# A state-space layer and two MLPs in one kernel: some decay matrices by ScalarE's exponential, the opening units reordered, the whole order planned anew

## The chip, the cores and the metric

One core of a Trainium2 chip runs the kernel. Its engines are TensorE (PE, matmul; PEld is its weight load), VectorE (DVE), ScalarE (ACT) and GpSimd (POOL); SyncE (SP) issues nearly all DMA transfers. The metric is device time in microseconds (us) of one execution, smaller is better.

## What is computed

```python
# 4 batches x 8 heads x 768 steps, head_dim 32, state 16, chunks of 32
L = np.exp(cum[:, :, :, None] - cum[:, :, None, :]) * causal   # cum: running sum of log a
y_intra = einsum('bhij,bhjd->bhid', (C @ B.T) * L, x)
y_inter = einsum('bhin,bhnd->bhid', C, state) * np.exp(cum)[..., None]
state = decay_full * state + sum(B x decay_from_j)
...
xn = x / sqrt(mean(x * x) + 1e-6) * rms_g              # 3072 tokens x 256
x = (silu(xn @ w_gate) * (xn @ w_val)) @ w_out         # d_ff 1536
out = softplus(x @ w_in) @ w_out2                      # d_ff 2048
```

All of it is in float32. Each product of the two MLPs is made from three matmuls on split operands: high part times high part, low times high, high times low.

## The kernel before

The state-space layer is cut into 24 *units* of 128 steps of one batch (8 heads each), four units to a *block* of 512 tokens; units 0 to 3 are block 0. A unit needs a decay matrix for each of its 8 heads (two tiles of 128 x 512, index `s`), which `unit` makes with a `tensor_tensor_scan` on DVE (L566: running products of `a`, restarted by a row of the identity). PE makes the unit's C·B scores into two PSUM banks of the tag `a` (`scores`), DVE multiplies them into the decays (`decay`, L615), PE makes the unit's output and new state (`products`), ACT squares it and scales it by the RMS gain, and `norm` makes 1/rms: a mean by PE (`msum`), a power by POOL, a broadcast by PE (`rspread`), a product on DVE (L783), then the split into high part (ACT, L358) and low part (DVE or POOL, L365). There are only two `a` banks, so the scores of the next unit wait for both decays of this one. For units 0 to 3 the values of `a` are spread over partitions by PE (`spread`, tiles `p<-st,small`) into a `p` bank; there are four of those, one of them held by the filler matmuls until the MLP begins.

Then comes SwiGLU on block 0 (f runs over 12 slices of 128 columns: `wg`, `wv` by `three_pass`, then `wo` in `back`), on block 1, the second MLP (`wi`, `wp`) on both, and so on over six blocks. One front of SwiGLU for one f is 12 matmuls of 512 columns. A weight chunk holds two values of f. It comes by DMA (`wr`) and is unpacked by ACT (`zz`, L447), DVE (L450), ACT (high part, L454) and DVE (low part, L456). Units 4 to 23 run between the matmuls of the MLPs.

Every operation is first recorded with a cost per engine (`Plan.op`). `Plan.emit` then runs a list scheduler twice. The first run is over the opening operations that carry a time by hand (table `LEAD`, `FIRST`); it yields times that they hold later. The second is over everything, by fixed ranks, and its order is the program's order on each engine. Idle time on PE before the MLP is filled with *filler* matmuls (`p<-mean`), which keep PE's clock up; their number and places are part of the fixed program order.

Of the kernel before, what the change touches and what calls it, by code (L numbers as in the profile page):

```python
# [26 lines left out]
NATIVE, SPREAD = 8, 4  # L27
NORMS = {0: [1, 1, 1, 1]}
# [11 lines left out]
FIRST = [(12.05, 14.4, 15.0, 17.3), (12.1, 15.2, 16.2, 20.4)]  # L40

LEAD = dict(
    spread0=(-0.6, 0.0, 2.6, 6.1), spread1=(-0.4, 1.5, 3.7, 9.6), scores=(-0.2, 4.9, 8.4, 12.1), products=(6.0, 9.5, 13.5, 15.3),
    msum=(7.9, 11.1, 15.2, 16.9), rspread=(9.55, 13.2, 17.3, 18.9),
    scan0=(0.0, 2.28, 5.75, 9.3), scan1=(1.14, 4.6, 8.1, 11.95), decay0=(3.4, 6.9, 10.4, 13.3), decay1=(4.0, 7.5, 11.0, 13.9),
    scale=(2.6, 6.0, 9.6, 13.1), norm=(11.6, 14.5, 18.3, 19.4),
    square=(7.3, 10.8, 14.5, 16.3), gains=(7.6, 11.1, 14.9, 16.6), mean=(8.7, 11.9, 16.15, 17.65), state=(8.8, 12.0, 17.7, 19.0),
    power=(8.9, 12.2, 17.3, 18.3), high=(12.2, 15.1, 18.9, 19.9), low=(12.9, 15.6, 18.8, 20.0))

W_LEAD, T0, U_LEAD, U_GAP, U_GAP0, U1, U1_GAP, B_LEAD, EPI = 50, 50, 115, 8, 4, 10, 14, 50, 40  # L50

SLIP = 100
# [25 lines left out]
class Plan:  # L78
# [3 lines left out]
    def __init__(self, latency):  # L82
        self.ops, self.bufs, self.latency = [], [], latency
        self.last_w, self.readers, self.seq = {}, {}, {}
        self.now = None
# [44 lines left out]
    def emit(self):  # L130
        lead = [i for i, o in enumerate(self.ops) if i in self.seq]
        due = {}
        self.run(lead, {}, due, True)
        for fn in self.run(range(len(self.ops)), due, {}):
            fn()

    def run(self, which, due, times, warm=False):
# [64 lines left out]
        while todo:  # L202
# [10 lines left out]
            for e in engines:  # L213
                able = []
                turn = lane[e][at[e]] if at[e] < len(lane[e]) else None
                for i in cand[e]:
                    if i in seq and i != turn:
                        continue
# [3 lines left out]
                    if i not in seq and turn is not None:  # L222
                        until = due[turn] + SLIP
                        if i in spare:
# [3 lines left out]
                    able.append((t, i not in seq, ops[i][1], i))  # L228
                while able:
# [3 lines left out]
                    end = t + ops[i][0][e][0]  # L233

                    later = False
                    for e2, way in ops[i][0].items():
                        if e2 != e:
                            ns, t2 = way[0], start(i, e2)
                            t2 += sum(ops[j][0][e2][0] for j in cand[e2]
                                      if len(ops[j][0]) == 1 and ops[j][1] < rank and ready[j] <= t2)  # L240
# [9 lines left out]
            times[i] = t  # L250
            for e2 in ops[i][0]:
                cand[e2].discard(i)
            if i in seq:
                at[e] += 1
            end = t + ns
# [34 lines left out]
def tile_ssd_then_swiglu_then_softplus_mlp(  # L290
# [84 lines left out]
    cst_sb = const.tile([P, -(-(sbuf_at // 4 + P + 1 + KD) // 64) * 64 - sbuf_at // 4], F32, name="cst_sb")  # L375
    ident4 = const.tile([P, 4 * P], F32, name="ident4")
    ident = ident4[:, 0:P]
    mask = cst_sb[:, 0:P]
    zeros = cst_sb[:, P:P + 1].to_broadcast([P, P])
    small = const.tile([P, 64], F32, name="small")  # L380
    g_sb, mhalf = cst_sb[:, P + 1:P + 1 + KD], small[:, 0:1]
    mean = const.tile([P, 64], F32, name="mean")[:, 0:1]
    sel = small[:, 4 * SPREAD:8 * SPREAD].bitcast(F32R)
# [693 lines left out]
```

## Time and profile before

| | us |
|---|---|
| runs of the kernel: median of three | 603.28 (601.46 to 604.17) |
| the profiled execution, its own time | 604.33 |
| its span, first to last instruction | 601.3 |
| PE busy in the span | 595.0 |
| DVE, ACT busy | 351.2, 309.5 |
| first MLP matmul starts at | 30.03 |

PE's instructions follow each other nearly without a gap, so "busy" does not say how much of it is useful: fillers count as busy, and so does a matmul at half clock. In the rows, a matmul of 512 columns is shown as 0.38 us long, but the next starts after about 0.215.

### The profile page before, as it was taken

The numbers are of one execution on the slowest core, as the hardware profiler recorded it, in microseconds if no ns is written. First come the engines' busy times: TensorE is split into PE (matmuls) and PEld (weight loads), VectorE is DVE, ScalarE is ACT, GpSimd is POOL, SyncE is SP. The second block draws the span as 40 slices with busy tenths as digits, with TensorE's granted clock in tenths as the row PEclk, the third lists the DMA queues.
The fourth block names the chain that finished last, engine by engine and source line by source line (L and its number), as shares of the span: only waits on it lengthen the run. The fifth ranks groups of instructions, "written<-read, shape, count | busy, mean of one in ns | idle before, by whom it ended". The sixth has DMA issues, their size and how long they took to land.

```text
span 601.3 us, 8773 instructions
## 1 busy us (share of the span) xinstructions
PE 595.0 (99%) x3377; PEld 513.7 (85%) x3377; DVE 351.2 (58%) x561; ACT 309.5 (51%) x547; POOL 20.0 (3%) x41
## 2 busy tenths in 40 slices
PE   9999999999999999999999999999999999999997
PEld 7888888888888888888888888888888888888885
DVE  6899997888683246695433779755333433322222
ACT  2666665768565445354555344665433333644543
POOL 3300000000000000000000000000000000000000
PEclk9899999999999999999999999999999999999999
DMA  6567768476710015111346533300100000000000
GB/s 210 187 206 246 248 240 245 159 241 214 232 48 36 1 43 178 42 57 35 132 173 207 163 109 88 120 1 0 37 0 1 0 2 1 0 1 0 36 1 35
DMA packets 33433, 59.74 MB, mean 99 GB/s; under 512 B 3120, under 2 KB 14960, under 8 KB 33392
## 3 DMA queue, kind: packets, MB, share of 16 engines
q1 hardware_dynamic: 33248, 58.93, 30.1%
q8 instruction: 26, 0.43, 0.3%
q10 hardware_dynamic: 144, 0.26, 0.1%
q14 instruction: 15, 0.12, 0.1%
HBM read 47.45 MB, written 11.73 MB: 98 GB/s over the span
## 4 chain that ended last, share of the span: by engine, by line
PE 94%; DVE 3%; DMA 1%; issue 0%; ACT 0%; POOL 0%; DVEq 0%; ACTq 0%
PE p L322 53%; PE t L322 35%; PE a L322 6%; DMA wr<-in_w 1%; DVE hw L365 1%; DVE wr L450 0%; DVE s L834 0%; DVE ab L566 0%; DVE xxl L783 0%; POOL xxl L365 0%; DVE xc L730 0%; DVE xxl L615 0%; DVE wol L456 0%; DVE s L359 0%; DVE wvl L456 0%
## 5 line engine op out<-in xcount | busy, mean ns | idle before, releaser
L365 DVE TENSOR_TENSOR hw<-s,hw 128x512 fp32r<-128x512 f32 x164 | 112.8, 690 | 144.0 <-ACT hw L358 83.3
L358 ACT ACTIVATE hw<-s 128x512 fp32r<-128x512 f32 x164 | 103.0, 631 | 98.9 <-DVE s L834 73.5
L322 PE MATMUL t<-hw,wph 128*128 128x512 f32 x384 | 114.7, 380 | 0.1
L846 ACT ACTIVATE s<-p 128x512 f32<-128x512 f32 x96 | 56.8, 598 | 78.7 <-PE p L322 77.6
L834 DVE TENSOR_TENSOR s<-s,p 128x512 f32<-128x512 f32 x72 | 49.2, 684 | 60.9 <-PE p L322 54.7
L322 PE MATMUL t<-hw,woh 128*128 128x512 f32 x272 | 82.3, 383 | 1.0 <-DVE hw L365 0.9
L322 PEld LDWEIGHTS t<-hw,wph 128*128 128x128 f32 x384 | 72.3, 189 | 11.0 <-ACT hw L358 0.5
L322 PE MATMUL p<-xxh,wih 128*128 128x512 f32 x192 | 72.8, 379 | 0.0
L322 PE MATMUL p<-xxl,wih 128*128 128x512 f32 x192 | 72.8, 379 | 0.0
L322 PE MATMUL p<-xxh,wil 128*128 128x512 f32 x192 | 72.8, 379 | 0.0
L322 PE MATMUL t<-hw,wpl 128*128 128x512 f32 x192 | 72.8, 379 | 0.0
L830 ACT ACTIVATE s<-p 128x512 f32<-128x512 f32 x72 | 42.8, 594 | 49.3 <-PE p L322 43.6
L322 PEld LDWEIGHTS t<-hw,woh 128*128 128x128 f32 x272 | 50.6, 189 | 9.8 <-DVE hw L365 1.8
L322 PE MATMUL p<-xxh,wgh 128*128 128x512 f32 x144 | 55.0, 382 | 0.0
L322 PE MATMUL p<-xxh,wvh 128*128 128x512 f32 x144 | 54.9, 381 | 0.0
L322 PE MATMUL p<-xxh,wvl 128*128 128x512 f32 x144 | 54.6, 379 | 0.0
L322 PE MATMUL p<-xxl,wvh 128*128 128x512 f32 x144 | 54.6, 379 | 0.0
L322 PE MATMUL p<-xxh,wgl 128*128 128x512 f32 x144 | 54.6, 379 | 0.0
L322 PE MATMUL p<-xxl,wgh 128*128 128x512 f32 x144 | 54.6, 379 | 0.0
L322 PE MATMUL t<-hw,wol 128*128 128x512 f32 x136 | 51.5, 379 | 0.0
L566 DVE TENSOR_TENSOR_SCAN ab<-ab,ident 128x512 f32<-128x512 f32 x40 | 48.7, 1219 | 2.0 <-DMA ab<-a_clip 2.0
L322 PEld LDWEIGHTS p<-xxh,wil 128*128 128x128 f32 x192 | 36.3, 189 | 5.1
(131 smaller groups left out, 753.3 us busy)
## 6 DMA issues: line engine op xcount, KB each, us to landing
wr<-in_w SPq DMA_DIRECT2D x34, 512.0 KB, 4.6
ab<-a_clip SPq DMA_DIRECT2D x20, 512.0 KB, 4.5
parts<-wr SPq DMA_DIRECT2D x16, 512.0 KB, 3.3
xc<-in_xc SPq DMA_DIRECT2D x20, 256.0 KB
st<-parts SPq DMA_DIRECT2D x16, 256.0 KB, 4.8
cz<-parts SPq DMA_DIRECT2D x32, 128.0 KB, 3.7
out_y<-s SPq DMA_DIRECT2D x11, 256.0 KB, 2.1
wr<-in_bc SPq DMA_DIRECT2D x8, 256.0 KB, 3.4
```

The costliest lines, as they stand in the source:

```text
L322: pe.matmul(out=o, lhsT=l, rhs=r, start=start, stop=stop, skip_group_check=True)
L358: ways = {"act": (act_ns(n), lambda: act.activation(out=out(), in_=in_(), func=ACTF.Copy)), "dve": (dve_ns(n, sbuf), lambda: dve.tensor_co ...
L365: return lambda: eng.tensor_tensor(out=out(), in0=in_(), in1=f32(hi()), op=ALU.subtract)
L566: DVE(512, rank[0], lambda t=t, d=d: dve.tensor_tensor_scan(out=t(), data0=d(), data1=ident4, initial=0.0, op0=ALU.mult, op1=ALU.add), dk ...
L830: ACT(n, rank - EPI, lambda: act.activation(out=s()[:, 0:n], in_=ps[0]()[:, 0:n], func=ACTF.Silu), [ps[0]], [s, "table"] if new_table else ...
L834: DVE(n, rank - EPI, lambda: dve.tensor_tensor(out=s()[:, 0:n], in0=s()[:, 0:n], in1=ps[1]()[:, 0:n], op=ALU.mult), [s, ps[1]], [s], port= ...
L846: ACT(n, rank - EPI, lambda: act.activation(out=s()[:, 0:n], in_=hp()[:, 0:n], func=ACTF.Softplus), [hp], [s, "table"] if new_table and f ...
```

## The change

- **Exponentials.** For five of the eight decay tiles of units 0 to 3 (`EXPS`: the second tile of units 0, 1 and 2, both of unit 3) the scan on DVE and the spread on PE go. In their place the logarithms of `a` are taken once (ACT, Ln), summed along the steps by one short scan (DVE), split into high and low parts, and PE makes for each tile all differences of sums in one `p` bank (`differences`: one matmul of 512 columns, four of 128, one of 512 with bf16 operands that puts -4096 where the matrix has to be zero). ACT takes Exp of it, 128 x 512.
- **Loads and tables.** Two small loads of `a` and the load of the constants are issued from ACT's queue, no longer SP's. The table loaded first holds Ln and Exp; the one with Silu is loaded at the end of the lead (one load more in all).
- **First units.** In the first run of the scheduler the times by hand no longer fix the order: of two operations that compete for an engine the one goes first whose order gives the shorter longest way to the end (`first`, `way`).
- **Whole order.** The second run is made eight times; after each, `refine` sets ranks anew from the due times of the MLP's matmuls, and the order with the earliest last matmul is kept.
- **Three passes.** `three_pass` now does high x high and high x low for both k first, low x high last. The number of MLP matmuls, 2448, stays.

```diff
+EXPS, NEVER = {(0, 1), (1, 1), (2, 1), (3, 0), (3, 1)}, -4096.0
...
+SILU = 15.0
+PASSES, MARGIN, MLP, DMA_WAIT = 8, 1.0, 768, 3000
...
+            for (_, old, n), (_, new, _) in zip(row, row[row[0][2]:]):
+                for i in old:
+                    after[i].add(new[0])
...
+        for _ in range(40):
+            for i in reversed(lead):
+                self.way[i] = ns[i] + max((self.way[j] + self.latency for j in after[i]), default=0.0)
         self.run(lead, {}, due, True)
-        for fn in self.run(range(len(self.ops)), due, {}):
+        self.seq = dict(due)
+        best = None
+        for _ in range(PASSES):
+            times = {}
+            order = self.run(range(len(self.ops)), due, times)
+            end = max(times[i] for i in times if "pe" in self.ops[i][0] and self.ops[i][1] < SPARE)
+            if best is None or end < best[0]:
+                best = end, order
+            self.refine(times)
+        for fn in best[1]:
             fn()
...
+            if "pe" in ops[i][0] and ops[i][1] < SPARE and i not in self.seq:
+                if free is not None:
+                    lost += max(0.0, times[i] - free)
+                free = times[i] + ops[i][0]["pe"][0]
+                if ops[i][4] >= MLP:
+                    due[i] = times[i] - lost
...
+            if i not in due or late.get(i, 1e9) - ns < due[i]:
+                due[i] = min(late.get(i, 1e9), held.get(e, 1e9)) - ns
+            held[e] = due[i]
+            for d in ops[i][2]:
+                late[d] = min(late.get(d, 1e9), due[i] - MARGIN * self.latency - (DMA_WAIT if self.on[d] in ("sp", "actq") else 0))
+        self.rank = {i: due.get(i, 1e9) if ops[i][1] < SPARE else 1e12 for i in range(len(ops))}
...
+    def first(self, i, t, j, t2, e):
+
+        a, b = (self.ops[k][0][e][0] for k in (i, j))
+        ij = max(t + self.way[i], max(t + a, t2) + self.way[j])
+        ji = max(t2 + self.way[j], t2 + b + self.way[i])
+        return ji < ij
...
+                    if warm and e not in queues and any(self.first(i, t, j, t2, e) for t2, _, _, j in able if t2 < end and j != i):
+                        able.remove(least)
+                        continue
...
-    ident = ident4[:, 0:P]
+    cst_sb = const.tile([P, -(-(sbuf_at // 4 + P + P // 2 + 1 + KD) // 64) * 64 - sbuf_at // 4], F32, name="cst_sb")
+    ident = const.tile([P, P], F32, name="ident")
+    ident4 = const.tile([P, 4 * P], BF16, name="ident4")
...
+            if (u, s) in EXPS:
+                def differences(s=s, d=d):
+                    r = u * NH + 4 * s
+                    mm(d()[:, :], c_hl(), minus[:, r:r + 4].rearrange("p (h i) -> p h i", i=1).to_broadcast([P, 4, P]), True, False)
+                    for k in range(4):
+                        mm(d()[:, k * P:(k + 1) * P], plus[:, r + k:r + k + 1].to_broadcast([P, P]), c_hl(), False, False)
+                    mm(d()[:, :], ident4[:, 0:P], never.rearrange("p (h i) -> p h i", h=1).to_broadcast([P, 4, P]), False, True)
+                PE(870, rank[0], differences, [ck, "plus", "minus", "cst", "ident"], [d], 1536)
+                at(f"scan{s}")
+                ACT(512, rank[0], lambda t=t, d=d: act.activation(out=t(), in_=d(), func=ACTF.Exp), dk + ["table"], [tk])
+                continue
...
             mm(o, a, swap(xh[:, k, 0:n]), k == 0, False)
-            mm(o, a, swap(xl[:, k, 0:n]), False, False)
-            mm(o, b, swap(xh[:, k, 0:n]), False, k == KD - 1)
+            mm(o, b, swap(xh[:, k, 0:n]), False, False)
+        for k in range(KD):
+            mm(o, W[wt][0][:, f, k], swap(xl[:, k, 0:n]), False, k == KD - 1)
...
-        plan.op({"act": (1283, lambda: act.preload_act_table_set("silu_and_others"))}, -200, (), ["table"])
+        plan.op({"act": (1283, lambda: act.preload_act_table_set("natural_log_exp_and_others"))}, -200, (), ["table"])
...
+        logs, c_hl = (lambda b=b: (b(), b.tile)[1][:, 2 * P:3 * P] for b in (raw4, a_hl))
+        lk, ck = (raw4, "c"), (a_hl, "c")
+        rowsc = [slice(64 * i, 64 * i + 8 * SPREAD) for i in range(2)]
...
+        for i in range(2):
+            plan.now = LOADS - 12 + i
+            plan.op({"actq": (16 * DMA_NS, lambda i=i: act.dma_start(out=logs()[rowsc[i]], in_=ab[0:SPREAD].rearrange("u o (h i) -> (u o h) i", i=P)))},
+                    -110, [lk], [(raw4, "c", i)])
...
+        POOL(32, -102, lambda: pool.tensor_tensor(out=plus, in0=ident[:, 0:8 * SPREAD], in1=ident[:, 64:64 + 8 * SPREAD], op=ALU.add), ["eye"], ["plus"])
+        POOL(32, -102, lambda: pool.tensor_scalar(out=minus, in0=f32(plus), scalar1=-1.0, scalar2=None, op0=ALU.mult), ["plus"], ["minus"])
...
+        DVE(128, -102, lambda: dve.tensor_scalar(out=logs(), in0=logs(), scalar1=1.0, scalar2=1e-6, op0=ALU.min, op1=ALU.max),
+            [(raw4, "c", 0), (raw4, "c", 1), lk], [lk])
+        ACT(128, -102, lambda: act.activation(out=logs(), in_=logs(), func=ACTF.Ln), [lk, "table"], [lk])
+        DVE(128, -102, lambda: dve.tensor_tensor_scan(out=logs(), data0=one.to_broadcast([P, P]), data1=logs(), initial=0.0,
+            op0=ALU.mult, op1=ALU.add), [lk, "one"], [lk], ns=300)
+        ACT(128, -102, lambda: act.activation(out=c_hl(), in_=logs(), func=ACTF.Copy), [lk], [ck])
+        plan.now = 6.9
+        DVE(128, -102, lambda: dve.tensor_tensor(out=c_hl()[64:P], in0=logs()[64:P], in1=f32(c_hl()[64:P]), op=ALU.subtract), [lk, ck], [ck])
...
+        plan.now = LOADS - 9
+        plan.op({"actq": (192 * DMA_NS, lambda: act.dma_start(out=cst_sb[:, 0:P + P // 2 + 1 + KD], in_=cst))}, -109, (), ["cst", "g"])
...
+            if u == SPREAD - 1:
+                plan.now = SILU
+                plan.op({"act": (1283, lambda: act.preload_act_table_set("silu_and_others"))}, -70, (), ["table"])
...
+    never = (NEVER * (np.arange(P)[:, None] > np.arange(P))).astype(np.float32).view(np.uint16)[:, 1::2]
+    cst[:, P + 1 + KD:] = np.ascontiguousarray(never).view(np.float32)
```

On PE the last stretch before the first MLP matmul (`p<-xxh,wgh`) is this in the program before; `t<-s`, `t<-xxl,s` are the products of unit 3, `p<-mean,xxh` an msum, `p<-ident_68,rs` an rspread, `a<-hw` the scores of unit 4, `p<-mean` fillers:

```order
L322 MATMUL p<-mean 128x512 x4
L322 MATMUL p<-mean,xxh 128x1 x2
L322 MATMUL t<-s 32x64 x4
L322 MATMUL t<-xxl,s 32x128 x8
L322 MATMUL p<-mean 128x512 x4
L322 MATMUL p<-mean,xxh 128x1 x2
L322 MATMUL p<-ident_68,rs 128x128
L322 MATMUL a<-hw 128x128 x8
L322 MATMUL p<-mean 128x512
L322 MATMUL p<-ident_68,rs 128x128
L322 MATMUL p<-mean 128x512 x9
L322 MATMUL p<-xxh,wgh 128x512
```

and this in the changed one, up to the row before that matmul; ahead of it stand the scores of unit 3 and the products of unit 2:

```order
L391 MATMUL p<-ident,rs 128x128
L391 MATMUL p<-mean 128x512 x3
L391 MATMUL p<-mean,xxh 128x1 x2
L391 MATMUL t<-s 32x64 x4
L391 MATMUL t<-xxl,s 32x128 x8
L391 MATMUL p<-mean 128x512 x3
L391 MATMUL p<-ident,rs 128x128
L391 MATMUL p<-mean,xxh 128x1 x2
L391 MATMUL p<-mean 128x512 x6
L391 MATMUL p<-ident,rs 128x128
L391 MATMUL a<-hw 128x128 x8
L391 MATMUL p<-mean 128x512 x4
```

The scores of unit 4 and the normalization's small matmuls keep their order among themselves; the fillers of the stretch are 16 in place of 18. In the whole lead there are 35 fillers, where there were 48. Further ahead, PE's row has between the scores of unit 2 and those of unit 3: the products of unit 1, both differences of unit 3, an rspread, and the msum of unit 1. That msum writes a `p` bank which the norm of unit 0 frees on DVE, and this norm now stands behind unit 2's decays and two weight instructions (L450 before, L522 now).

On DVE, behind the low part of the last unit of block 0 (`xxl<-xxl,xxh`), the program before has this; L566 is a scan of unit 4 or 5 (such rows print a scan as SCALAR_TENSOR_TENSOR), L450 and L456 the weight instructions, `wgl` the low part of the chunk for f = 2 and 3:

```order
L365 TENSOR_TENSOR xxl<-xxl,xxh 128x2x128
L456 SCALAR_TENSOR_TENSOR wvl<-wr,wvh 128x512
L566 SCALAR_TENSOR_TENSOR ab<-ab,ident_68 128x512
L450 SCALAR_TENSOR_TENSOR wr<-wr,zz_74 128x512
L566 SCALAR_TENSOR_TENSOR ab<-ab,ident_68 128x512
L456 SCALAR_TENSOR_TENSOR wgl<-wr,wgh 128x512
L834 TENSOR_TENSOR s<-s,p 128x512
```

The changed one has this (L650 is the scan, L522 and L528 the weight instructions, L920 the product of silu and value):

```order
L434 TENSOR_TENSOR xxl<-xxl,xxh 128x2x128
L528 SCALAR_TENSOR_TENSOR wol<-wr,woh 128x512
L650 SCALAR_TENSOR_TENSOR ab<-ab,ident_69 128x512 x3
L522 SCALAR_TENSOR_TENSOR wr<-wr,zz_75 128x512
L920 TENSOR_TENSOR s<-s,p 128x512
L670 TENSOR_TENSOR xc<-xc,ab 128x128
L650 SCALAR_TENSOR_TENSOR ab<-ab,ident_69 128x512
L528 SCALAR_TENSOR_TENSOR wgl<-wr,wgh 128x512
```

Between the low part and that `wgl` stood two scans and two weight instructions; now four scans, two weight instructions, a product and a small instruction stand there.

On PE near the end of block 4's SwiGLU, behind the last front (`wv` of f = 11), the program before has this, with `a<-cz_72,st` the scores of a unit:

```order
L322 MATMUL p<-xxh,wvh 128x512
L322 MATMUL p<-xxl,wvh 128x512
L322 MATMUL p<-xxh,wvl 128x512
L322 MATMUL t<-hw,woh 128x512 x2
L322 MATMUL t<-hw,wol 128x512
L322 MATMUL t<-hw,woh 128x512 x2
L322 MATMUL t<-hw,wol 128x512
L322 MATMUL a<-cz_72,st 128x256 x4
L322 MATMUL t<-hw,woh 128x512 x2
L322 MATMUL t<-hw,wol 128x512
L322 MATMUL t<-hw,woh 128x512 x2
L322 MATMUL t<-hw,wol 128x512
```

and the changed one this:

```order
L391 MATMUL p<-xxl,wvh 128x512 x2
L391 MATMUL t<-hw,woh 128x512 x2
L391 MATMUL t<-hw,wol 128x512
L391 MATMUL a<-cz_73,st 128x256 x4
L391 MATMUL t<-hw,woh 128x512 x2
L391 MATMUL t<-hw,wol 128x512
L391 MATMUL t<-hw,woh 128x512 x2
L391 MATMUL t<-hw,wol 128x512
L391 MATMUL t<-hw,woh 128x512 x2
L391 MATMUL t<-hw,wol 128x512
L391 MATMUL t<-hw,woh 128x512 x2
L391 MATMUL t<-hw,wol 128x512
```

Between the last front and the first matmul of the last slice's output there are now nine output matmuls besides the scores, where there were six.

## Rows read from the trace of the kernel before

**Rows 1.** The page: busy time, share of the span and instructions of each engine.
```profile
PE 595.0 (99%) x3377; PEld 513.7 (85%) x3377; DVE 351.2 (58%) x561; ACT 309.5 (51%) x547; POOL 20.0 (3%) x41
```

**Rows 2.** PE's timeline, lead: start, length, instruction, tiles, shape, count.
```profile
0.92 4.82 PE L322 MATMUL p<-mean 128*128 128x512 f32 x11 [0.92 <-DVE small L950]
...
17.92 1.16 PE L322 MATMUL a<-hw 16*128 16x128 f32 x16
19.01 0.48 PE L322 MATMUL p<-mean 128*128 128x512 f32 x1
19.33 0.39 PE L322 MATMUL p<-ident,rs 128*128 128x128 f32 x2
19.64 0.32 PE L322 MATMUL t<-s 128*32 128x64 f32 x8
...
20.33 1.14 PE L322 MATMUL p<-mean 128*128 128x512 f32 x4
21.31 0.50 PE L322 MATMUL p<-mean,xxh 128*128 128x1 f32 x4
21.74 0.32 PE L322 MATMUL t<-s 128*32 128x64 f32 x8
...
26.78 3.41 PE L322 MATMUL p<-mean 128*128 128x512 f32 x9
30.03 0.38 PE L322 MATMUL p<-xxh,wgh 128*128 128x512 f32 x1
30.25 0.38 PE L322 MATMUL p<-xxl,wgh 128*128 128x512 f32 x1
```

**Rows 3.** DVE's timeline, lead; in brackets the idle time before and what ended it.
```profile
3.44 0.28 DVE L927 TENSOR_SCALAR st<-st 64x256 f32<-64x256 f32 x1 [2.54 <-DMA st<-in_ab]
...
6.01 3.45 DVE L566 TENSOR_TENSOR_SCAN ab<-p,ident 128x512 f32<-128x512 f32 x3 [1.23 <-PE p L322]
9.38 1.26 DVE L615 TENSOR_TENSOR ab<-ab,a 128x512 f32<-128x512 f32 x2
...
19.71 1.29 DVE L615 TENSOR_TENSOR xxl<-xxl,a 128x512 f32<-128x512 f32 x2
...
27.16 0.42 DVE L783 TENSOR_TENSOR xxl<-xxl,p 128x256 f32<-128x256 f32 x1 [0.82 <-PE p L322]
...
28.13 0.43 DVE L365 TENSOR_TENSOR xxl<-xxl,xxh 128x256 fp32r<-128x256 f32 x1
...
32.70 0.69 DVE L456 SCALAR_TENSOR_TENSOR wgl<-wr,wgh 128x512 fp32r<-128x512 f32 x1 [0.69 <-ACT wgh L454]
```

**Rows 4.** Stretches: busy time of each engine, then granted clock, DMA share and GB/s.
```profile
25.85:29.25 3.40, 3.40 (x13) 2.80 (x10) 2.58 (x7) 1.87 (x5) 0.00 (x0) 0.50 0.33 109
30.00:90.00 60.00, 59.76 (x402) 49.60 (x402) 58.86 (x107) 41.30 (x78) 3.15 (x4) 1.00 0.71 236
```

**Rows 5.** ACT's timeline around a load of an activation table.
```profile
139.08 0.81 ACT L447 ACTIVATE zz<-wr 128x512 f16<-128x512 bf16 x1
139.90 1.28 ACT L846 ACT_TABLE_LOAD   x1
141.20 1.09 ACT L846 ACTIVATE s<-p 128x512 f32<-128x512 f32 x2
```

**Rows 6.** The page's groups: count, busy us, mean ns of one, idle time before.
```profile
L830 ACT ACTIVATE s<-p 128x512 f32<-128x512 f32 x72 | 42.8, 594 | 49.3 <-PE p L322 43.6
```

**Rows 7.** DVE's groups of the first 30 us, by shape.
```profile
L966 DVE TENSOR_TENSOR_SCAN s<-s,cst_sb 96x128 f32<-96x128 f32 x2 | 1.3, 670 | 0.0
```

**Rows 8.** PE's timeline at a wait in block 1's SwiGLU.
```profile
87.58 0.38 PE L322 MATMUL t<-hw,woh 128*128 128x512 f32 x1
88.20 0.48 PE L322 MATMUL t<-hw,woh 128*128 128x512 f32 x1 [0.24 <-DVE hw L365]
```

**Rows 9.** PE's timeline at a wait near the end of block 4's SwiGLU.
```profile
371.72 0.48 PE L322 MATMUL t<-hw,woh 128*128 128x512 f32 x1
372.86 0.48 PE L322 MATMUL t<-hw,woh 128*128 128x512 f32 x1 [0.66 <-DVE hw L365]
```

More of the change, by code (lines that the diff above doesn't have):

```diff
@@ L38 @@
 LOADS = -50.0
-FIRST = [(12.05, 14.4, 15.0, 17.3), (12.1, 15.2, 16.2, 20.4)]
+FIRST = [(11.7, 14.1, 14.65, 16.5), (13.9, 15.45, 16.1, 18.2)]
 LEAD = dict(
[L43 to L48, printed above, removed]
+    spread0=(5.2, 6.4, 8.3, 13.0), spread1=(7.4, 8.6, 10.9, 13.1), scores=(5.5, 9.7, 12.1, 14.5), products=(9.9, 12.3, 14.7, 17.0),
+    msum=(11.8, 14.2, 16.6, 18.0), rspread=(13.2, 16.0, 17.8, 19.0),
+    scan0=(5.8, 7.0, 9.4, 14.0), scan1=(8.6, 9.8, 12.2, 14.1), decay0=(8.2, 10.6, 13.0, 15.4), decay1=(8.8, 11.2, 13.6, 16.0),
+    scale=(7.2, 8.2, 10.6, 14.2), norm=(14.0, 16.1, 18.5, 20.4),
+    square=(10.9, 13.3, 15.6, 18.0), gains=(11.2, 13.6, 15.9, 18.3), mean=(12.6, 14.5, 17.0, 18.6), state=(12.7, 14.6, 18.9, 20.0),
+    power=(12.8, 15.0, 17.3, 18.9), high=(14.6, 16.7, 19.0, 21.0), low=(15.0, 17.0, 19.4, 21.4))
 W_LEAD, T0, U_LEAD, U_GAP, U_GAP0, U1, U1_GAP, B_LEAD, EPI = 50, 50, 115, 8, 4, 10, 14, 50, 40
+SILU = 15.0
+PASSES, MARGIN, MLP, DMA_WAIT = 8, 1.0, 768, 3000
 SLIP = 100
@@ L131, in emit @@
         lead = [i for i, o in enumerate(self.ops) if i in self.seq]
-        due = {}
-        self.run(lead, {}, due, True)
-        for fn in self.run(range(len(self.ops)), due, {}):
-            fn()
+        self.rank = {i: o[1] for i, o in enumerate(self.ops)}
+        due, held, rows = {}, set(lead), {}
+        after = {i: {j for j in lead if i in self.ops[j][2]} for i in lead}
+        for b in self.bufs:
+            mine = [i for i in b.ops if i in held]
+            if mine:
+                rows.setdefault((b.pool, b.tag), []).append((self.seq[mine[0]], mine, b.bufs))
@@ new lines, in emit @@
+        for row in rows.values():
+            row.sort()
+            for (_, old, n), (_, new, _) in zip(row, row[row[0][2]:]):
+                for i in old:
+                    after[i].add(new[0])
+        ns = {i: min(w[0] for w in self.ops[i][0].values()) for i in lead}
+        self.way = dict(ns)
+        for _ in range(40):
+            for i in reversed(lead):
+                self.way[i] = ns[i] + max((self.way[j] + self.latency for j in after[i]), default=0.0)
+        self.run(lead, {}, due, True)
@@ L216, in run @@
                 for i in cand[e]:
-                    if i in seq and i != turn:
+                    if i in seq and i != turn and (not warm or e in queues):
                         continue
@@ L250, in run @@
             times[i] = t
+            self.on[i] = e
             for e2 in ops[i][0]:
@@ L383, in tile_ssd_then_swiglu_then_softplus_mlp @@
     sel = small[:, 4 * SPREAD:8 * SPREAD].bitcast(F32R)
+    plus, minus = (small[:, (2 + i) * 8 * SPREAD:(3 + i) * 8 * SPREAD].bitcast(F32R) for i in range(2))
+    one = small[:, 1:2]
+    never = cst_sb[:, P + 1 + KD:P + P // 2 + 1 + KD].bitcast(BF16)
     cz = [const.tile([P, 4, 2, P], F32, name=f"cz{i}") for i in range(2)]
```

54 lines of the change are left out of this document (37 added, 17 removed).

## Prediction

> **What bounds the kernel now.** The page says that PE is busy for 595.0 of 601.3 us [rows 1], so whatever gains must come out of PE's row: useless matmuls, waits, or matmuls at half clock. I read PE's timeline from the front to see where the useful part begins. The first MLP matmul starts at 30.03, the next 0.22 later [rows 2]; 2448 of them at 0.215 make 526, the same in both programs. So three things can move: the lead before that start, the waits behind it, and the small matmuls of units 4 to 23, which stay the same in number and shape.
>
> In the lead the reader is to see two engines. DVE works almost without a break from 6.01 on: three scans in 3.45 (1.12 from start to start), two decays in 1.26, and the last low part at 28.13 [rows 3]. PE is full as well, but of fillers: nine of them fill 26.78 to 30.03 [rows 2]. They take 3.25 and not the 1.94 that nine times 0.215 gives, because the granted clock is 0.50 from 25.85 to 29.25 [rows 4], that is 1.2 GHz in place of 2.4. The last low part ends at 28.56 [rows 3], so the MLP starts 1.47 later than its data allow: the order is fixed, and the nine fillers have to run.
>
> Behind the lead DVE is the crowded engine (58.86 of 60 us between 30 and 90), and yet PE hardly waits there (59.76 busy) [rows 4]. The waits that I find are two: at 87.58 two matmuls lie 0.62 apart, 0.40 too much [rows 8]; at 371.72 it is 1.14, 0.92 too much [rows 9]. Both end with a DVE low part.
>
> **The change part by part.**
>
> *DVE's relief.* Five scans of 1.12 go: 5.6. Added are a clip, a scan and a subtraction on 128 columns. The small scan I bound by a quarter of a large one, 0.28, and by the scan of 128 columns in the trace, 0.67 [rows 7]; I take 0.35, and 0.2 each for the others by the clip of 256 columns, 0.28 [rows 3]. Net 4.8 less. That would be the gain if DVE alone set the lead. It does not, as the chain shows.
>
> *The chain of the lead.* I follow the changed order with durations from the rows. Ten fillers at about 0.43 from 0.92 on end at 5.2 [rows 2]. Next on PE are now unit 0's scores, 1.1 at full clock [rows 2] and up to twice that at half, then the spread: DVE's first scan starts at about 7.0 (6.01 before). Two scans and two decays end at 10.6. Unit 1's scores need both `a` banks, so they wait for that; PE has its two tiles of differences and two fillers in between, and starts them at 11.4. Decays of unit 1: 12.6 to 13.8. Products 0.69, fillers 0.98, msum 0.43 [rows 2] bring unit 2's scores to 14.7, its decays to 17.1. Then DVE has two weight instructions, 1.2 (of 0.69 each, overlapping a little [rows 3]), and unit 0's norm, and only then can the msum go that stands on PE ahead of unit 3's scores: they start at 19.2 and end at 20.3, decays 20.4 to 21.6. Before they were 19.71 to 20.9 [rows 3]. So the last decays do not come sooner at all; the scans' time has turned into waits for scores.
>
> From the end of those scores PE's row is (durations from rows 2, start to start): products 0.69, rspread 0.31, three fillers 0.77, msum 0.43, products 0.69, fillers 0.77, rspread 0.31, msum 0.43, six fillers 1.41, rspread 0.31, scores 1.09, four fillers 0.98; together 8.2, so the MLP starts at 28.5. The norm behind the last rspread starts at 26.5, and norm, high and low part took 1.4 before (27.16 to 28.56 [rows 3]): the data are there at 27.9 to 28.4, so the fillers decide, barely. That is 1.5 sooner than 30.03, nearly all of it the half clock that I assume away. Bounds: 27.9, if the small steps cost 0.05 less each, and 29.2. **Term 1: -1.5.**
>
> *A new wait.* Four groups of six matmuls come before f = 2; the 26th matmul needs the low part `wgl`. PE is there at 28.5 + 25 x 0.215 = 33.9. Before, this `wgl` stood at 32.70 to 33.39 [rows 3], PE came at 30.03 + 26 x 0.215 = 35.6, and 2.2 us of slack covered it. Now DVE has between the low part (start about 27.6) and the end of `wgl`: 0.34, a weight instruction 0.6, three scans 3.36, 0.6, the product 0.6, 0.2, a scan 1.12, and itself 0.69, together 7.5: 35.1. Everything else on PE is queued behind that matmul. Bounds: nothing, if DVE runs 1.2 earlier against PE, and 1.7. I take 1.3, since the low part and PE's start hang on the same rspread and shift together. **Term 2: +1.3.** DVE's saved time is what was spent here: scans of units 4 and 5 were pulled in front of a weight.
>
> *Old waits.* By 87.58 DVE has less left to do than before (its scans of units 4 to 7 came sooner), so 0.4 goes. At 371.72 three more matmuls stand ahead of the late low part, 0.65 of cover; 0.27 stays. **Term 3: -1.05**, between 0 and -1.3.
>
> *At nothing.* Five Exp on ACT from PSUM: the nearest row is Silu on the same shape, 594 ns [rows 6]; 3.0 in all in a lead where ACT has room, and a decay waits for its bank's scores longer than for its Exp. The matmuls of differences: 1536 columns, 0.65 by columns, perhaps 0.9 with six starts, in place of spreads and fillers. Logarithms: their loads come from ACT's queue behind the first table load (1.28 [rows 5]); SP's load of `a` was there at 3.44 [rows 3], so I put these at 4.4 and five small steps of some 0.35 later, at 6.2, while PE reaches the differences at 7.3 (5.2, scores 1.5, spread 0.6). That cover is 1.1; each us beyond it costs one. The order of `three_pass` alone moves nothing: same matmuls, the low part four matmuls later. Silu's table load, 1.28 [rows 5], lies on ACT behind the third unit's high part, while PE and DVE still make the last norm.
>
> The Trainium skill ("ScalarE: Activation LUTs", What ACT_TABLE_LOAD costs) puts a switch at 1283 ns plus a drain of about 1380 ns. Here the row shows 1.28, the activation before ending at 139.89, the next starting at 141.20 [rows 5]: the trace has the first part and not the second.
>
> **Sum.** -1.5 + 1.3 - 1.05 = -1.25 against the profiled execution's own 604.33: 603.1. This execution is 1.05 above the median of the runs. I carry 0.8 of that over (part of what separates executions may be the clock's fall, which term 1 already removes) and say **602.3**, 0.2% under the median.
>
> **The rivals.** Half a per cent, 3.0 us, is about what a measurement of this kernel can tell from no change; so faster means under 600.3 and slower over 606.3.
>
> 1. *The new wait does not come and the start is early.* If the third and fourth pulled-in scans fit beside the weight, term 2 is 0, and with the start at 28.0 (another 0.5) and the rest of the old waits gone (0.25) the profiled execution is 601.05, the median 600.2. For it: DVE has 4.8 less to do, and PE waited hardly at all while DVE was full [rows 4]. Against it: the rows stand on DVE in that order, and their durations leave no gap. Chance 0.22.
>
> 2. *The clock falls where work stands* (the other side). The lead has 35 fillers instead of 48, and PE now stands idle or sparse around 9, 17 and 22 to 26. In the rows the clock fell to 1.2 GHz once, behind a stretch of small matmuls, and it hit fillers [rows 2, 4]. A fall of the same length on the scores, differences and products doubles up to 3.4 of work that is on the chain: +1.7, since half of it is work, each time, and the waits of DVE add to it. One fall gives 604 to 605; two or three, with term 3 gone, 606.5 and more, and from there it decides. Chance 0.13 for one at least, 0.07 for slower.
>
> The Trainium skill ("TensorE: Matmul & The Clock Gate", What's actually happening) says that the activity window is free-running and does not restart with a kernel, so a fall would hit the same program in some executions only. The three times before, 2.7 apart, fit that; one trace can't show it.
>
> 3. *The table switch costs about as much again.* If ACT stood still for another 1.3 behind Silu's load (a second 1.28), the last high part would come at 28.5, the low part's end at 29.0, and the MLP would start 0.5 later than in term 1: 602.8. Against it: the next activation starts 0.02 behind the load [rows 5]. Chance 0.02.
>
> That standstill is what the rule of the Trainium skill cited above ("ScalarE: Activation LUTs") would make of this load.
>
> 4. *The logarithms are late.* Loads from ACT's queue land over 1 us later than I think, all decays shift, 604 and up. Chance 0.04.
>
> **Chances.** The forecast as summed, 600.4 to 604, has 0.59. Faster by over 0.5%: 0.21. Slower: 0.10 (rival 2's worse half and a little from 4). Within: 0.69. The range 599.6 to 605.4 leaves out about 0.09 on either side.
>
> **What would show it.** Right: the first MLP matmul at 27.9 to 29.2 with a granted clock of 1.00 before it; last decays of unit 3 ending after 20.9; a PE wait of about 1.3 on the second `wgl` near 34, `wgl`'s DVE instruction right behind a scan; DVE idle for some us in the lead. Wrong: no wait there (rival 1); a stretch at 0.50 between 6 and 26 (rival 2); a gap above 0.1 between the table load and the next activation (rival 3); PE waiting for ACT or DVE at 7 (rival 4).

## The result, and the profile after

The changed kernel takes 606.08 us (median of 10, 603.32 to 610.25), the kernel before 602.46 on the same chip (median of 10): ratio 1.0067, 95% interval 1.0050 to 1.0084. It is slower by 0.67%, where 602.3 was forecast. The profiled execution of the changed kernel took 605.5, its span is 603.7. Against [rows 1], the page says:

```profile
PE 594.7 (99%) x3383; PEld 513.6 (85%) x3383; DVE 348.6 (58%) x560; ACT 315.1 (52%) x555; POOL 20.9 (3%) x44
```

DVE's busy time fell by 2.6 and not by the 4.8 of the prediction, because two short instructions stood longer there (below). ACT's rose by 5.6: five exponentials make 3.0 of that, one table load more 1.28. Neither sum explains the loss, so I read PE's timeline, as [rows 2, 8, 9] (in brackets the idle time before, and what ended it):

```profile
0.94 3.96 PE L391 MATMUL p<-mean 128*128 128x512 f32 x10 [0.94 <-DVE small L1059]
4.90 1.36 PE L391 MATMUL a<-hw 16*128 16x128 f32 x16
7.12 0.90 PE L391 MATMUL p<-st,small 128*128 128x256 f32 x4 [0.86 <-DVE st L1026]
...
20.98 0.58 PE L391 MATMUL p<-mean,xxh 128*128 128x1 f32 x4 [0.60 <-DVE xxl L867]
...
29.52 1.14 PE L391 MATMUL p<-mean 128*128 128x512 f32 x4
30.49 0.38 PE L391 MATMUL p<-xxh,wgh 128*128 128x512 f32 x1
...
35.78 0.48 PE L391 MATMUL p<-xxh,wgh 128*128 128x512 f32 x1
37.29 0.48 PE L391 MATMUL p<-xxh,wgl 128*128 128x512 f32 x1 [1.02 <-DVE wgl L528]
...
81.11 0.59 PE L391 MATMUL p<-xxl,wgh 128*128 128x512 f32 x2
81.89 0.82 PE L391 MATMUL a<-ident,rs 128*128 128x128 f32 x5 [0.18 <-DVE rs L841]
...
374.01 0.38 PE L391 MATMUL t<-hw,woh 128*128 128x512 f32 x1
374.59 0.48 PE L391 MATMUL t<-hw,woh 128*128 128x512 f32 x1 [0.20 <-DVE hw L434]
```

The first MLP matmul starts at 30.49 (28.5 forecast). PE waits 0.86 ahead of 7.12 for DVE, 0.60 ahead of 20.98, and for the second `wgl` as forecast. What DVE did before 7.12 is in its timeline, against [rows 3]:

```profile
3.37 2.36 DVE L1032 TENSOR_SCALAR st<-st 128x128 f32<-128x128 f32 x1 [2.46 <-DMA st<-in_ab]
3.54 2.32 DVE L1022 TENSOR_SCALAR st<-st 64x256 f32<-64x256 f32 x1
...
6.10 0.43 DVE L1035 TENSOR_TENSOR_SCAN st<-small,st 128x128 f32<-128x128 f32 x1
6.56 0.41 DVE L1026 TENSOR_TENSOR st<-st 16x256 fp32r<-16x256 f32 x1
7.00 0.29 DVE L1039 TENSOR_TENSOR st<-st 64x128 fp32r<-64x128 f32 x1
7.63 2.34 DVE L650 TENSOR_TENSOR_SCAN ab<-p,ident 128x512 f32<-128x512 f32 x2 [0.34 <-PE p L391]
...
22.68 1.29 DVE L699 TENSOR_TENSOR xxl<-xxl,a 128x512 f32<-128x512 f32 x2 [1.56 <-PE a L391]
...
30.68 3.45 DVE L650 TENSOR_TENSOR_SCAN ab<-ab,ident 128x512 f32<-128x512 f32 x3
...
36.56 0.67 DVE L528 SCALAR_TENSOR_TENSOR wgl<-wr,wgh 128x512 fp32r<-128x512 f32 x1
```

A *clip* holds the values of `a` between 1e-6 and 1. L1032 is the new clip, of the logarithms' input; L1022 is the clip of the spreads' input, which was there before: 0.28 in [rows 3], 2.32 here, in the same shape. The wait of 0.86 is for L1026, the low part of the spreads' input, which follows that clip; the sums of logarithms are split by 7.29 (L1039). The loads were in time. What else ran then is in POOL's timeline:

```profile
3.34 0.52 POOL L1062 MEMSET zz<- 128x512 f32 x1
3.81 1.84 POOL L1065 MEMSET cz<- 128x1024 f32 x2
```

POOL fills buffers with zeros (*memsets*), `zz` for the weights and `cz` for later units, from 3.34 to 5.65, and the clips end at 5.73 and 5.86. In the kernel before, POOL did this at 8.78 (`zz`) and 12.21 (`cz`), beside a scan that kept its 1.22. The change touches no memset, but this line of the scheduler's first run:

```diff
-                    if i in seq and i != turn:
+                    if i in seq and i != turn and (not warm or e in queues):
```

Times by hand no longer hold POOL back, and the memsets have no inputs to wait for (argued from the code; this line alone was not tried). Last, the granted clock in stretches, as [rows 4]:

```profile
7.47:10.88 3.41, 3.41 (x15) 3.05 (x14) 2.40 (x3) 0.60 (x1) 0.41 (x1) 0.50 0.92 278
10.90:30.00 19.10, 18.50 (x230) 15.71 (x229) 12.57 (x25) 13.29 (x35) 6.87 (x11) 1.00 0.69 221
```

Right behind the wait of 0.86 the clock is at 1.2 GHz for 3.41, on spreads and differences.

### The profile page after: what moved, and what is told of

Same layout as the page of the kernel before. It is cut to its first block, busy times and chain, and to the rows that moved or that the text cites. A ratio compares the mean times of both kernels' runs of the same rounds, so it can differ in the third digit from the quotient of the medians.

```text
span 603.7 us, 8788 instructions
## 1 busy us (share of the span) xinstructions
PE 594.7 (99%) x3383; PEld 513.6 (85%) x3383; DVE 348.6 (58%) x560; ACT 315.1 (52%) x555; POOL 20.9 (3%) x44
## 4 chain that ended last, share of the span: by engine, by line
PE 94%; DVE 4%; DMA 1%; ACT 1%; issue 0%; DVEq 0%; ACTq 0%; SPq 0%
PE p L391 52%; PE t L391 36%; PE a L391 6%; DMA wr<-in_w 1%; DVE ab L650 0%; DVE s L920 0%; DVE st L1032 0%; DVE hw L434 0%; DMA st<-in_ab 0%; DVE xxh L813 0%; DVE xxl L867 0%; DVE xc L814 0%; ACT L1101 0%; DVE ab L699 0%; ACT xxh L427 0%
## 5 line engine op out<-in xcount | busy, mean ns | idle before, releaser
L920 DVE TENSOR_TENSOR s<-s,p 128x512 f32<-128x512 f32 x72 | 49.2, 684 | 66.6 <-PE p L391 60.9
L391 PE MATMUL p<-xxl,wih 128*128 128x512 f32 x192 | 57.1, 379 | 0.0
L650 DVE TENSOR_TENSOR_SCAN ab<-ab,ident 128x512 f32<-128x512 f32 x40 | 48.2, 1216 | 0.2 <-DMA ab<-a_clip 0.2
L391 PE MATMUL p<-xxl,wvh 128*128 128x512 f32 x144 | 42.8, 379 | 0.0
L391 PE MATMUL p<-xxl,wgh 128*128 128x512 f32 x144 | 42.8, 379 | 0.0
L391 PEld LDWEIGHTS p<-xxh,wih 128*128 128x128 f32 x192 | 36.3, 189 | 5.2 <-issue 0.2
```

The lines of the kernel that those rows point to most:

```text
L391: pe.matmul(out=o, lhsT=l, rhs=r, start=start, stop=stop, skip_group_check=True)
L650: DVE(512, rank[0], lambda t=t, d=d: dve.tensor_tensor_scan(out=t(), data0=d(), data1=ident4, initial=0.0, op0=ALU.mult, op1=ALU.add), dk ...
L920: DVE(n, rank - EPI, lambda: dve.tensor_tensor(out=s()[:, 0:n], in0=s()[:, 0:n], in1=ps[1]()[:, 0:n], op=ALU.mult), [s, ps[1]], [s], port= ...
```

## Experiments

My theory: the memsets beside the clips cost the time, by the wait, by the order that was planned around them, and by the clock. Rivals: the thinner row of PE (fewer fillers, so that PE stands idle for short times) costs the clock by itself; the eight passes cost it behind the lead (the new wait). But for a second profile of the changed kernel, the experiments ran in three sets, each on another chip with the kernel before beside it, which had medians of 601.85, 602.21 and 602.29; a time is best compared with the one beside it. Three numbers of the profiles that the argument compares:

| kernel | first MLP matmul | last matmul starts | between |
|---|---|---|---|
| before, profile ahead of the prediction | 30.03 | 596.82 | 566.79 |
| before, longer code | 28.11 | 595.18 | 567.06 |
| changed, first and second profile | 30.49, 30.41 | 598.24, 597.88 | 567.75, 567.47 |
| memsets late | 29.28 | 596.31 | 567.03 |
| memsets late, planned | 28.26 | 596.02 | 567.76 |
| the same, one pass | 28.18 | 597.02 | 568.84 |
| the same as planned, memsets moved | 27.13 | 594.88 | 567.76 |
| and four fillers less | 26.00 | 594.68 | 568.68 |

**Memsets late.** In the finished order of the changed kernel one `zz` (row 25) and both `cz` go behind u1's scaling:

```diff
-        for fn in best[1]:
-            fn()
+        order = list(enumerate(best[1]))
+        for i, j in [(25, 76), (30, 76), (37, 76)]:
+            at = [k for k, _ in order]
+            row = order.pop(at.index(i))
+            order.insert([k for k, _ in order].index(j), row)
+        for _, fn in order:
+            fn()
```

> The changed kernel with three POOL memsets (one zz, two cz) moved behind the second scaling of u1; nothing else moves. Collision theory (the two clips on VectorE stood from 3.37 to 5.86 because POOL wrote those memsets from 3.34 to 5.65): both clips take about 0.3 and end by 4.0, the first row of spreads starts by 5.8 instead of 7.12, the granted clock is not at half between 7.5 and 10.9, the first MLP matmul comes at 28.5 to 29.1 instead of 30.49, and the time falls by 1.5 to 2, to 604.0 to 604.6. Thin-row theory (the thinner row of TensorE costs the clock whatever POOL does): clips short, but a half-clock stretch stands in the lead all the same, first MLP matmul 29.5 to 30.5, time 605.4 to 606.1.

604.60 (602.41 to 609.64), ratio 1.0046 (1.0025 to 1.0066). DVE's and PE's timeline, and the stretch that was at half clock:

```profile
3.40 0.23 DVE L1037 TENSOR_SCALAR st<-st 128x128 f32<-128x128 f32 x1 [2.49 <-POOL small L1035]
3.56 0.28 DVE L1027 TENSOR_SCALAR st<-st 64x256 f32<-64x256 f32 x1
```
```profile
6.77 0.73 PE L396 MATMUL p<-st,small 128*128 128x256 f32 x4
...
19.77 0.58 PE L396 MATMUL p<-mean,xxh 128*128 128x1 f32 x4 [0.60 <-DVE xxl L872]
...
29.28 0.38 PE L396 MATMUL p<-xxh,wgh 128*128 128x512 f32 x1
```
```profile
7.47:10.88 3.41, 3.02 (x20) 2.36 (x19) 3.41 (x5) 0.62 (x2) 0.41 (x1) 1.00 0.87 284
```

The clips are short again with nothing moved but the memsets, so the collision is shown. The median is 1.5 lower than the 606.08 of another set, as expected; against the kernel before beside each it is 0.9 lower (3.62 above it, then 2.75), and the intervals of the two ratios overlap. Two things did not follow the theory. The spreads start at 6.77 and not by 5.8, behind the scores of unit 0 (u0), and the first MLP matmul at 29.28, not by 29.1: that order was planned around the memsets and stays. And of the 12 executions 8 have a mean granted clock of 0.997 or less (0.986 in the slowest), spans 601.6 to 607.6; three undisturbed ones have 600.6 to 600.7. So the clock falls without the collision too: both theories hold half.

**The collision in the kernel before.** There only `cz` is made early, by its time and one read (one filler more comes with it):

```diff
-        plan.now = 6.1
+        plan.now = LOADS + 2
...
-            POOL(370, -1 + i, lambda i=i: pool.memset(cz[i], 0.0), (), [("zero", i)])
+            POOL(370, -1 + i, lambda i=i: pool.memset(cz[i], 0.0), ["sel"], [("zero", i)])
```

> The kernel before with its two cz memsets on POOL moved ahead, right behind the small addition that ends at 2.90; the only other difference is one filler more. Collision theory: the memsets take 2.9 to 4.75, the clip that took 0.28 at 3.44 ends at 4.8, the first scan starts at 7.0 to 7.1 instead of 6.01, the first MLP matmul comes 1.0 to 1.3 later (31.0 to 31.3) and the time rises by 1 or more, to 603.5 to 604.5. Without a collision: clip 0.28, time 602.0 to 603.0.

602.75 against 601.85, ratio 1.0012 (1.0002 to 1.0023). DVE's clip, and POOL:

```profile
3.52 1.20 DVE L927 TENSOR_SCALAR st<-st 64x256 f32<-64x256 f32 x1 [2.62 <-DMA st<-in_ab]
```
```profile
2.74 1.84 POOL L956 MEMSET cz<- 128x1024 f32 x2
```

The clip is stretched in the same way and ends behind the last memset (4.58, the clip 4.72), in a kernel without exponentials. The time is where I expected it without a collision, 0.9 above the kernel before: the first MLP matmul is at 28.96, not at 31, because my expectation added to 30.03, and 28.11 is the start without a half-clock stretch (in the profile of the kernel before with the longer code, below).

**The second `wgl`.** In the changed kernel the four steps of that weight go ahead of scans (order[197], [200], [204] before the first of the four, order[192], and [211] before the third, order[198], by the same loop).

> The changed kernel with the four steps of the second wg weight (two on ScalarE, two on VectorE) moved ahead of the scans that stood in front of them; nothing else moves. If the wait at 37.29 is only that order: the gap of 1.51 between the first wgh and the first wgl matmul of f=2 closes to 0.22, and the time falls by 1.3, to 604.8. If something else takes its place (the scans, now later, hold up the products of the second block): the gap closes, a new wait of about the same length stands within the next 10 us, time 605.8 to 606.3.

604.31, ratio 1.0043 (1.0027 to 1.0058). PE's timeline:

```profile
36.19 0.38 PE L396 MATMUL p<-xxh,wgh 128*128 128x512 f32 x1
36.41 0.38 PE L396 MATMUL p<-xxh,wgl 128*128 128x512 f32 x1
...
37.49 0.38 PE L396 MATMUL t<-hw,woh 128*128 128x512 f32 x1
39.00 0.48 PE L396 MATMUL t<-hw,woh 128*128 128x512 f32 x1 [1.14 <-DVE hw L439]
```

The gap at the weight is closed, and 1.51 from one matmul to the next stand a few matmuls later at the hidden tile (`hw`, the split product of silu and value). The median fell, but all six executions have a mean clock of 0.997, and at that clock the changed kernel has a span of 601.9 (one execution), this one 601.7 to 602.6: nothing gained. So I moved the two scans of u5 behind the hidden tile as well, on top of the memsets:

> The changed kernel with the memsets late, the second wg weight's steps ahead as in the run of that kind, and the two scans of u5 moved behind the second half of the first hidden tile; nothing else moves. If VectorE's row from 30 to 39 is overfull because of four scans in front (the wait went from the wgl to the hidden tile when only the weight was moved): the gaps of 1.5 close at both places, and the time is 1.3 below the run with the memsets late alone: 603.3. If another wait takes their place again: 604.3 to 604.9.

603.99 (602.72 to 610.50), ratio 1.0041 (1.0017 to 1.0065). Both gaps are gone from the waits, and the spans of the six executions with a mean clock of 0.999 are 600.9 to 601.4, against 600.6 to 600.7 with the memsets late alone. The expected 1.3 did not come; where it goes is not settled (PE waits 0.37 for a decay at 41.6, and more small gaps behind it).

**The end of the program.** In the changed kernel's first profile the last matmul starts 5.5 ahead of the span's end, in the others 4.3 to 4.5. A packet of instructions (16384 B) comes while the output is written; the DMA view of 599 to 600 has it (packets, MB, share of 16 engines):

```profile
q8 instruction: 1, 0.02, 7.6%
```

To put it there in the kernel before, eight short matmuls follow the last ones, into a PSUM buffer of their own (m is 0 and 1):

```diff
+                        for _ in range(8 * m):
+                            mm(xp()[:, 0:64], mean.to_broadcast([P, P]).bitcast(F32R), mean.to_broadcast([P, 64]).bitcast(F32R), True, True)
...
+            xp = pbuf("a", [P, 4 * P])
...
```

> The kernel before with eight short matmuls (128x64) behind the last real matmul; nothing waits for them and no output comes from them. Code theory (in the changed kernel a packet of instructions of 16384 B is fetched at 599.58, while the last output is written, and the last transfer ends 2.97 after its issue; before, 1.97 after it, with that packet at 603.59, behind the end): the packet now falls into the writing of the output, the last transfer ends about 3.0 after its issue and the time rises by 1.0, to 603.4. If the longer end of the changed kernel was chance: last transfer ends 1.9 to 2.1 after its issue, time 602.2 to 602.9.

601.98 against 601.85, ratio 1.0002 (0.9990 to 1.0015). The packet came at 595.16, ahead of the output, so this run didn't test it. A second profile of the changed kernel did:

> The changed kernel once more, for a second profile. Of its end: in the first profile a packet of instructions of 16384 B is fetched at 599.58, 0.20 behind the last output transfer's issue, and that transfer ends 2.97 after its issue; in the run of the longer code the packet came at 595.16, ahead of the output, and cost nothing. If the place of the packet is fixed by the program, it falls into the output again and the last transfer ends 2.9 to 3.0 after its issue; if not, 1.9 to 2.1. Of the clock: a half-clock stretch somewhere between 7 and 30 again, not necessarily at 7.5 to 10.9, since the mean granted clock differed from execution to execution. Of the collision, which has no chance in it: both clips end again at 5.6 to 5.9, right behind the last cz memset.

604.02 in one execution, against 602.00 beside it. The packet came at 602.78, the last transfer ended 1.97 behind its issue: the 1.0 at the end of the first profile was chance, and so is as much of the 2.4 between the two spans, 601.3 and 603.7 (the first MLP matmul makes 0.46 of these, the stretch to the last matmul 0.96). The collision was there again (clips 3.35 to 5.76), and so was the half clock, 7.58 to 10.99.

**The order planned without the early memsets.** The three memsets read the split sums (`ck`), and everything is planned anew; the second kernel sets `PASSES` to 1, the third `EXPS` to the empty set:

```diff
-            POOL(180, -103, lambda i=i: pool.memset(zz[i], 0.0), (), [("zz", i)])
+            POOL(180, -103, lambda i=i: pool.memset(zz[i], 0.0), [ck] if i else (), [("zz", i)])
...
-            POOL(370, -1 + i, lambda i=i: pool.memset(cz[i], 0.0), (), [("zero", i)])
+            POOL(370, -1 + i, lambda i=i: pool.memset(cz[i], 0.0), [ck], [("zero", i)])
```

> The changed kernel whose three POOL memsets (one zz, two cz) read the split sums, so that they come behind them, and whose whole order is planned anew with that: TensorE now has the first spreads and differences ahead of the scores of u0. Against the run with only the memsets moved (median 604.6, first MLP matmul 29.28 in a profile without a half-clock stretch): if the scores of u0, which stood in front of the spreads, were the next thing on the path, the spreads start at 5.3 to 5.6 instead of 6.77, the first MLP matmul comes at 28.0 to 28.4, and the time is 602.2 to 603.5. If the clock of the thin row decides: the same lead, but most executions with a half-clock stretch, 604 to 605.

> As the run above, but the whole order planned once instead of eight times. The lead is the same, instruction by instruction. If the eight passes cost time behind the lead (waits of the kind of the second wgl): 0.5 to 1.3 faster than the run above. If they give what they are for: 0.3 to 1 slower. Otherwise the same within 0.3.

> As the first of these runs, but all eight first decay matrices by scans (the logarithms are still made and not used): 45 to 50 fillers in the lead again instead of 36. If the exponentials with their thin row of TensorE cost the time: few half-clock stretches, first MLP matmul 28.0 to 28.5, time 601.2 to 602.2. If the planning of the whole order costs it: 603 or more also here.

602.24 (602.02 to 603.22), ratio 0.9997 (0.9986 to 1.0009); 603.42, ratio 1.0018 (1.0007 to 1.0029); 609.27, ratio 1.0111 (1.0092 to 1.0129). So the loss is gone with this order; the passes gain 1.2; and with scans for all tiles the same planning loses 7.0 (61 fillers, first MLP matmul 29.22, waits of 0.7 to 1.1 for weights and hidden tiles until 62; these explain only a part). The exponentials do not cost the time: all 11 executions of the first have a mean clock of 0.998 or more, with 34 fillers. But its clips were still long, DVE and POOL, and PE waited for them, longer than in the changed kernel:

```profile
3.62 1.28 DVE L1032 TENSOR_SCALAR st<-st 128x128 f32<-128x128 f32 x1 [2.71 <-DMA st<-in_ab]
3.79 1.24 DVE L1022 TENSOR_SCALAR st<-st 64x256 f32<-64x256 f32 x1
```
```profile
3.41 0.52 POOL L1062 MEMSET zz<- 128x512 f32 x1
3.88 0.94 POOL L1065 MEMSET cz<- 128x1024 f32 x1
```
```profile
6.30 0.70 PE L391 MATMUL p<-st,small 128*128 128x256 f32 x4 [1.13 <-DVE st L1026]
```

One `zz` and one `cz` still stand beside the clips: the read moved the memsets in the plan, and POOL does not wait for it. So it is the order that took the loss away here, not an end of the collision. In this order the msum of unit 1 (u1) follows the rspread without a gap; and in spite of the wait of 1.13 none of the 11 executions has a fall of the clock. With the three rows moved behind u1's scaling in the finished order (the other `cz` among them), and then without the last four fillers:

> The kernel of the run with the memsets planned late (median 602.24), whose profile shows that POOL did not wait: zz stood at 3.41 and a cz at 3.88 to 4.82, and the clips still took 1.28 and 1.24 and ended by 5.03. Here the three memsets stand on POOL behind the second scaling (u1); nothing else moves. Collision theory: clips 0.23 and 0.28, first spreads at 5.2 to 5.5 instead of 6.30, first MLP matmul 27.1 to 27.4 instead of 28.26, time 601.0 to 601.5, which is 0.1 to 0.2% under the kernel before. If TensorE's own row (fillers, the rise of the clock) sets the lead: first MLP matmul 27.9 to 28.3, time 602.0 to 602.4.

> As the run above, without the four fillers that stand in front of the first MLP matmul (27.28 to 28.26 in the profile of the planned run, while its first operand, xxh, was ready at 27.23). If they only stand in the way: first MLP matmul 0.7 to 0.9 earlier than in the run above, time 0.7 to 0.9 lower, about 600.4. If the clock needs them: half-clock stretches in many executions, time the same or higher than above.

601.42 (600.92 to 602.25), ratio **0.9979** (0.9967 to 0.9992), and 601.39, ratio 0.9988 (0.9977 to 0.9998). The first is a little faster than both kernels; the spreads start at 5.25, the first MLP matmul at 27.13. Without the four fillers it starts at 26.00, and nothing is gained: the stretch up to the last matmul is 0.92 longer. The waits of PE for the hidden tile (total, times, longest), with and without the four fillers:

```profile
PE t L396 <- DVE hw L439: 1.7, 3, 1.0
PE t L397 <- DVE hw L440: 2.5, 3, 1.3
```

What the lead gives is lost again in waits for DVE behind it.

**The gap.** The memsets late as in the first run, and three fillers in PE's gap of 0.60 in front of u1's msum:

```diff
+        at = [k for k, _ in order].index(114)
+        order[at:at] = [order[[k for k, _ in order].index(7)]] * 3
```

> The changed kernel with the memsets moved, as in the first run of that kind (median 604.6; 8 of its 12 executions with a mean granted clock of 0.997 or less), and three fillers in TensorE's gap of 0.60 at 19.2 to 19.8, in front of the sum that waits there for VectorE. If that gap is what the clock falls on: a mean clock of 0.999 or more in at least 9 of 12 executions, median 602.4 to 603.2. If the falls have another cause: still half or more of the executions with a fall, median 604 to 605.

602.27 (601.52 to 605.54), ratio 1.0006 (0.9991 to 1.0022). None of 12 executions has a mean clock under 0.998; with the gap it was 8 of 12, and 3 of 12 in the run with u5's scans behind, whose lead is the same. Two profiles show where such a fall stands. With u5's scans behind, the half clock is at 20.92 to 27.74, behind a wait of 0.61 that ends at 19.09. With the weights ahead, where the same msum starts at 19.94 after 0.60, it is here:

```profile
22.52:25.93 3.41, 3.41 (x34) 2.71 (x32) 2.54 (x5) 2.00 (x7) 0.87 (x2) 0.50 0.99 316
```

Three fillers took 2.3 off the median of another set (604.60), and 2.8 against the kernel before beside each. In two executions (605.5, span 603.7, mean clock 1.0) something else cost about 3: in the profiled one PE works at half pace until about 13.9 (four spreads at 7.51 take 1.22 there, at 6.77 in the first run 0.73; four short matmuls take 0.95 at 12.28 and 0.56 at 13.89). Why is open; the runs with the memsets late and with u5's scans behind have one and two executions like them, 603.6 to 604.2 at a mean clock of 1.0.

## Why the prediction was wrong, by its own steps

- **Term 1, its base.** "-1.5 ... nearly all of it the half clock that I assume away": 30.03 holds a stretch at half clock that most executions of the kernel before don't have (in the three sets 6, 8 and 9 of 29 have a mean clock under 0.998). Without it the start is 28.11. The same fall was taken off again with the 0.8 between profile and median. From 28.11 and the median 602.46 my own terms give 602.46 + 0.4 + 1.3 - 1.05 = 603.1.
- **Term 1, its chain.** This is the step that failed, with the cover for the logarithms that it put "at nothing". It took the inputs of PE's first spreads and differences as there in time, and the clock as full. The new clip was priced at 0.2 and took 2.36, the old one 2.32 and not 0.28. The sums were split at 7.29, not at 6.2, and the low part that the spreads need was there only at 6.97, so PE waited 0.86. Right behind that wait 3.41 went by at a granted clock of 0.50, on work of the chain. Unit 1's scores started at 13.24 (11.4 in the chain), the first MLP matmul at 30.49 and 30.41 (28.5). I read no row of POOL, although the order moved its memsets. Rivals 4 (late logarithms, by another cause than late loads) and 2 (the clock on work that stands) came together; each alone had its price, the two together had none. Rival 2 had a chance of 0.13, and 9 of the 10 executions of the changed kernel have a mean clock of 0.997 or less.
- **Rival 2's reason.** Not the number of fillers as such: 34 of them did without a fall in the planned order (the lead has 35 in the changed kernel; before, the trace has 49, not 48). The gap in front of u1's msum, which the chain had ("only then can the msum go"), was counted as time, 0.6, and not as clock. What makes a wait end in a fall is open: 1.13 ahead of the spreads did not in the planned order, 0.86 did in the changed one. The runs bear out that a fall hits one program in some executions only: mean clocks of the changed kernel go from 0.986 to 0.999. The prediction had drawn that from the Trainium skill ("TensorE: Matmul & The Clock Gate", What's actually happening), whose activity window does not start with the kernel.
- **Term 2** was right in place and size: from one matmul to the next 1.51 and not 0.22, 1.29 too much, 1.3 forecast (its sum, 35.1 less 33.9, gives 1.2). Its reading was too narrow: moving the weight ahead only moved the wait to the hidden tile, so DVE had too much to do there, not one weight too late.
- **Term 3** was right in kind: the wait at 87.58 is gone, 0.36 stays at 374.01 (0.27 forecast), and a new wait of 0.35 stands at 81.11. Together -0.6, forecast -1.05.
- **DVE's relief, ACT, table.** The scan's time did turn into waits for scores (decays of u3 at 22.68 behind 1.56 idle). An activation starts 0.02 behind the table load of 1.28, here too, so rival 3 did not come:

```profile
27.43 1.28 ACT L1101 ACT_TABLE_LOAD   x1
28.73 0.68 ACT L526 ACTIVATE woh<-wr 128x512 fp32r<-128x512 f32 x1
```

What the loss of 3.6 is made of, each median against the kernel before beside it: 3.62 above it in the changed kernel, 2.75 with the memsets late, 0.02 below it with the gap filled too, 0.87 below it with the planned order and its memsets moved. So the collision alone costs 0.9. Two other pairs say the same: the kernel before with its own memsets early (0.90 above), and the planned order with its memsets moved or not (0.87 below, 0.03 above). Each 0.9 by itself is at the edge of the noise; the three agree. The gap and the clock behind it make 2.8, and the place of u0's scores with the rest of the new plan 0.9, by which the best of these kernels is under the kernel before. The second share is the least sure: with u5's scans behind, and the same gap, the median was only 1.78 above the kernel before. It was also not tried to fill the gap and leave the memsets early, and in both profiles of the changed kernel the half clock stands behind the collision's wait, ahead of this gap.

## What to carry to other kernels

Before a gain is forecast from a profile, take out what only that execution shows (a stretch at half clock on idle work), or the change is credited with it. When an order is planned anew, read every engine's row, also that of one that is busy for 3%: an instruction without inputs moves to where nothing holds it, and may stand beside the one short step that all else waits for. A gap in a thin row can cost more by the clock than by its length (2.8 against 0.6 here, though a wait of 1.13 elsewhere brought no fall); fillers in it were cheap.

## What the runs showed of the hardware

- A clip (TENSOR_SCALAR, one input, f32, 128x128 or 64x256) takes 0.23 to 0.29 alone and stands beside a POOL memset until that is over: up to 2.36, 1.28 and 1.20 in three kernels. The Trainium skill ("SBUF — State Buffer", Who interferes with whom) has this rule: a `tensor_scalar` in a two-port mode and POOL lock the same ports, and the one that starts second is blocked for the whole instruction of the other. The trace agrees, though it does not show the clip's mode, and goes further: the clip that started beside `zz` (3.41 to 3.93) also stood through the `cz` behind it (3.88 to 4.82) and ended at 4.90. It was blocked for POOL's whole run of memsets, not for one.
- A scan with one input in PSUM and one in SBUF kept its 1.22 beside such memsets (from 12.00 on, `cz` from 12.21 to 14.05, in the kernel before).
- In the one execution where a packet of instructions came while the output was written, the last transfer ended 2.97 after its issue instead of 1.97; in a second execution of the same program the packet came later and the transfer ended after 1.97.
